# Weighing the values by half blocks of 64 keys from the fourth batch on

## The chip, the cores and the metric
One core of one Trainium2 chip. The metric is the device time of one execution in microseconds (us), the median of three runs.

## What is computed
Attention with a causal window of 128 keys and a linear bias by distance, for 8 batches, 8 heads, 576 positions and 64 features a head, and then an MLP with GELU over all 4608 positions.

```python
scores = scale * np.matmul(q, k.transpose(0, 1, 3, 2))
mask = (rel >= 0) & (rel < window)                  # window = 128, rel = query - key
scores = np.where(mask, scores + bias[None], -1000000000.0)
attn = np.exp(scores - max); attn = attn / (sum + 1e-09)
x = np.matmul(attn, v)                              # (4608, 512) after the heads are joined
h = x @ w_in                                        # 512 x 2048
return (0.5 * h * (1.0 + erf(h * inv_sqrt2))) @ w_out   # 2048 x 512
```

## The kernel before
The positions are taken in nine tiles of 512 tokens (`TT`); a batch has 576, so batch b fills the end of tile b and the beginning of tile b+1. Most products are made from pairs of 16-bit parts, high and low, in three terms: (high, high), (high, low), (low, high).

**Attention.** A unit is one batch and one pair of heads (`Unit`; four pairs a batch). Queries go in nine blocks j of 64 (`QB`), each of which sees the key blocks j-2, j-1 and j. The rows of a unit stand in nine groups (`GROUPS`): five of even blocks (`EVEN`), four of odd ones (`ODD`). `scores` (matmuls of L415) fills five PSUM banks of the ring `att`, which has four buffers; DVE (L437) reads them with the bias into `s`. `softmax` makes, for the even groups and then for the odd ones, the maximum (DVE L507), the exponential (ACT L510), the normalised weights as a high part (POOL L519) and a low part (DVE L149, the helper `low_part`) in `e_main`, and one transposing DMA on SP's queue (L522) into `et`. Weights stand in `et` as two slots of 128 keys for each group: an even block j has its keys j-2 and j-1 in slot 0, its own keys in the lower half of slot 1, and zeros in the upper half; an odd block has j-2 in the upper half of slot 0, zeros below, and j-1 and j in slot 1.

`weigh` multiplies `et` with the values. It goes over the two tiles that the batch touches (blocks 0 to 7-b for tile b, blocks 8-b to 8 for tile b+1), with one `att` bank for each. For every block of 128 keys and slot there is one matmul a head: the values are the stationary 128 rows x 64 columns, the two heads go to the two halves of the columns, and where two neighbouring blocks j share it, they go together:

```python
for slot, j0 in ((1, 2 * kb), (0, 2 * kb + 2)):
    js = [j for j in (j0, j0 + 1) if j in blocks]
```

So a unit has 54 to 66 matmuls of 128 or 64 columns (L559). Then, for each tile, ACT reads the bank into the high part of the tile `x` (L572) and DVE makes the low part (L573, at the helper's line L149).

**MLP.** `mlp_in` (L600) makes the 16 blocks of h from x, 12 matmuls each; GELU by ACT (L623) into `g32`, of the ring `ob` with three buffers; the high part by POOL (L625) and the low part by DVE (L149). `mlp_out` (L661) makes four blocks of 128 tokens, 48 matmuls each. Both use the PSUM ring `mm` of four banks.

**Order.** The main loop runs over the tiles t = 1 to 7 in 32 steps (16 of `mlp_in`, 16 of `mlp_out`) and puts the attention of batch t+1 into them: `SCORES_AT, WEIGH_AT = (2, 11, 16, 21), (12, 20, 25, 30)`. At step 24 `split_qk` splits the next q and k, at step 1 of the next tile `split_v` splits V (ACT L337, DVE L149), and the loads and maxima of the batch after (`load_v`, `stat_v`, `split_qk`; DVE L217) follow. A scheduler then sets the final order on every engine by its own model of time, so a step can end some matmuls off its place. Tile 8 is made by another scheme (`seven_all`).

Of the kernel before, what the change touches and what calls it, by code (L numbers as in the profile page):

```python
# [11 lines left out]
F32 = mybir.dt.float32  # L12
I32 = mybir.dt.int32
U32 = mybir.dt.uint32
AF = mybir.ActivationFunctionType
# [3 lines left out]
B, H, S, D = 8, 8, 576, 64  # L19
WINDOW = 128  # L20
P = 128
QB = 64
NB = S // QB
# [4 lines left out]
TT = 512  # L28
# [6 lines left out]
NKB = 5  # L35
# [13 lines left out]
NEVEN = 5  # L49
# [8 lines left out]
def attention_gelu_mlp(  # L58
# [10 lines left out]
    nc = tc.nc  # L69
    pool = ctx.enter_context(tc.tile_pool(name="sb", bufs=1))  # L70
    dram = ctx.enter_context(tc.tile_pool(name="dram", bufs=1, space=bass.MemoryType.DRAM))
    psum = ctx.enter_context(tc.tile_pool(name="ps", bufs=1, space=bass.MemoryType.PSUM))

    def small(shape, name, bufs, tag=None, dt=F32):
        return pool.tile(shape, dt, tag=tag or name, name=name, bufs=bufs)
# [8 lines left out]
    ident, upper, never = (adders[:, n] for n in range(3))  # L84
# [63 lines left out]
    def low_part(dst, src, scale, high):  # L148
        nc.vector.scalar_tensor_tensor(  # L149
            out=dst, in0=src, scalar=scale, in1=high, op0=ALU.mult, op1=ALU.subtract  # L150
        )
# [139 lines left out]
    def x_tile(t):  # L291
        if t not in xt:
            xt[t] = pool.tile([P, NCC, 2, TT], F16, tag="x", name=f"x{t}", bufs=2)
        return xt[t]
# [7 lines left out]
    vbuf = pool.tile([P, 2, NPAIR, NKB, P], F16, name="vbuf")  # L302

    pwv, scv, pwx, sx, cx = {}, {}, {}, {}, {}
# [229 lines left out]
    def weigh(st):  # L534

        b, hp, et = st.b, st.hp, st.et
        first = NB - 1 - b
        for t, blocks in ((b, range(0, first)), (b + 1, range(first, NB))):
            av = psum.tile([P, TT], F32, tag="att" if b else "mm", name=f"av{st.u}_{t}", bufs=4)
            jobs = []  # L540
            for kb in range(NKB):
                for slot, j0 in ((1, 2 * kb), (0, 2 * kb + 2)):
                    js = [j for j in (j0, j0 + 1) if j in blocks]
                    if js:
                        jobs.append((kb, slot, js))
            terms = ((None, 0),) if b < EXACT else ((0, 0), (0, 1), (1, 0))
            k = 1 if b < EXACT else 2
            todo = [(vi, ei, job) for vi, ei in terms for job in jobs]
            for n, (vi, ei, (kb, slot, js)) in enumerate(todo):
                for h in range(2):  # L550
                    r = slice(h * D, h * D + D)
                    j = js[0]
                    half = (j // 2) % 2
                    g = 4 if j == 8 else (NEVEN if j % 2 else 0) + 2 * h + j // 4
                    if j == 8:
                        half = h
                    base = et[:, (g * k + ei) * 2 + slot, half * QB : half * QB + QB]
                    steps = [[NEVEN * 2 * k * P, 2]] if len(js) == 2 else []
                    nc.tensor.matmul(  # L559
                        av[r, (j - blocks[0]) * QB : (j - blocks[0] + len(js)) * QB],  # L560
                        v32s[b][:, hp, kb, r] if b < EXACT else vbuf[:, vi, hp, kb, r],
                        bass.AP(tensor=base.tensor, offset=base.offset, ap=[list(base.ap[0])] + steps + [[1, QB]]),
                        start=(n == 0), stop=(n == len(todo) - 1), skip_group_check=True,
                    )
            n = len(blocks) * QB
            at = b * S + blocks[0] * QB - t * TT
            if b == 0 and t == 1:
                nc.scalar.copy(tail[:, hp], av[:, :n])
                continue
            x = x_tile(t)[:, hp, :, at : at + n]  # L570
            c = sx[t] if b < EXACT else cx[b, t] if t < B else cx_last
            nc.scalar.activation(x[:, 0], av[:, :n], AF.Copy, scale=c)  # L572
            low_part(x[:, 1], av[:, :n], c, x[:, 0])  # L573


    g_of = {}
# [415 lines left out]
    cx_last = None  # L992
# [5 lines left out]
    for hp in range(NPAIR):  # L998
        turn(unit(0, hp))
        if hp + 1 < NPAIR:  # L1000
            softmax_first(unit(0, hp + 1))
        if hp == 0:
            stat_v(0)
        if hp + 2 < NPAIR:
            all_scores(unit(0, hp + 2))
        weigh(unit(0, hp))
# [3 lines left out]
    for n in range(0, NWP, 2):  # L1010
        g = gates[n // 2]
# [30 lines left out]
    todo = [(m, whole, 0, NFC - 1) for m in range(NWP)]  # L1042
# [3 lines left out]
    for n, (m, tbs, first, last) in enumerate(todo):  # L1046
        for fc in (2 * m, 2 * m + 1):
            for tb in tbs:
                mlp_out(0, tb, fc, first, last)
        if n in split_at:  # L1050
            weights_out_split(split_at[n])
        if n == 2:
            stat_v(2)
        if n in scores_at:
            all_scores(unit(1, scores_at[n]))
            softmax(unit(1, scores_at[n]))
        if n in weigh_at:
            weigh(unit(1, weigh_at[n]))
# [9 lines left out]
    for t in range(1, NTILE):  # L1068
        b = t + 1
        scores_at, weigh_at = (SCORES_AT, WEIGH_AT) if t > 1 else ((8, 14, 18, 22), (17, 22, 26, 30))  # L1070
        at = {s + i: (hp, i) for hp, s in enumerate(scores_at) for i in range(3)}
# [5 lines left out]
        for step in range(2 * NFC):  # L1077
            if step < NFC:
                mlp_in(t, step)
            else:  # L1080
                tb, q = divmod(step - NFC, 4)
# [11 lines left out]
            if step in at:  # L1093
                hp, i = at[step]
# [8 lines left out]
            if step == 6:  # L1103
                if b + 1 < B:
                    stat_v(b + 1)
                else:
# [4 lines left out]
                    cx_last = small([P, 1], "cxl", 1)  # L1111
                    nc.vector.tensor_scalar(cx_last, pwv[B - 1], sx[B], 2.0 ** -27, op0=ALU.mult, op1=ALU.mult)
            if step in weigh_at:
                weigh(unit(b, weigh_at.index(step)))
# [43 lines left out]
```

## Time and profile before

| | us |
|---|---|
| median of 3 runs | 944.19 (943.04 to 946.74) |
| the profiled execution | 947.36 |
| its span, first to last instruction | 945.3 |
| PE busy | 909.2 |
| DVE busy | 720.3 |
| ACT busy | 546.5 |
| POOL busy | 194.2 |

PE's busy time is the time in which at least one matmul is under way; matmuls overlap, so it says how long PE was not idle, not how well it was used. A line number is that of the kernel; L149 is a helper that makes the low part of many tiles, which are told apart by the names beside it. Idle time of an engine other than PE counts only where PE comes to wait for it.

### The profile page before, as it was taken

The page shows a single profiled execution, that of the slowest core. Times are in us where ns is not written, and L with a number is a line of the kernel's source. Part 1 is how long each engine was busy: PE and PEld are TensorE (multiplying, and loading weights), DVE is VectorE, ACT ScalarE, POOL GpSimd, SP SyncE. Part 2 cuts the span into 40 slices and gives each one's busy share as a digit, 9 for nine tenths or more (in the row PEclk, how much of TensorE's full clock was granted, in tenths as well). Part 3 has the DMA queues.
Part 4 walks back from the last instruction along what each step waited for, and adds up shares of the span by engine and source line. Part 5 has one row for each costly group of instructions (what it writes and reads, how often), then busy time and mean ns, then how long its engine had stood idle before and what let it go on. Part 6 is the DMA issues. An engine that isn't in the chain of part 4 may idle for free.

```text
span 945.3 us, 18563 instructions
## 1 busy us (share of the span) xinstructions
PE 909.2 (96%) x7356; PEld 475.2 (50%) x7356; DVE 720.3 (76%) x1445; ACT 546.5 (58%) x1146; POOL 194.2 (21%) x412
## 2 busy tenths in 40 slices
PE   6969999789999899999999999999999999999998
PEld 3544444444454345444454445444544444445887
DVE  6798989779876877678767877787656799991771
ACT  5977967776673565356435643564465526731760
POOL 1010000013101443135313531163125420000000
PEclk9889999999999999999999999999999999999999
DMA  9518532972446124614562346225302554300201
GB/s 317 212 45 259 209 105 67 203 191 61 90 126 165 36 57 83 187 43 79 96 162 68 62 101 174 69 51 99 86 13 51 91 116 146 90 34 23 79 24 45
DMA packets 185527, 99.63 MB, mean 105 GB/s; under 512 B 133344, under 2 KB 165216, under 8 KB 185312
## 3 DMA queue, kind: packets, MB, share of 16 engines
q1 hardware_dynamic: 185440, 98.45, 41.3%
q8 instruction: 57, 0.93, 0.4%
q14 instruction: 30, 0.25, 0.1%
HBM read 50.72 MB, written 13.63 MB: 68 GB/s over the span
## 4 chain that ended last, share of the span: by engine, by line
PE 68%; DVE 7%; ACT 5%; DMA 4%; issue 2%; SPq 1%; DVEq 0%; ACTq 0%
PE o L661 31%; PE h L600 22%; PE av L559 4%; PE sc L415 4%; DMA v<-vp 2%; PE u L789 2%; PE u_out L901 2%; PE v L789 2%; DMA et<-e_main 1%; ACT s L510 1%; DVE stv L217 1%; DVE vbuf L149 1%; DVE nmax L507 1%; ACT L623 1%; ACT vbuf L337 1%
## 5 line engine op out<-in xcount | busy, mean ns | idle before, releaser
L600 PE MATMUL h<-x,wi 128*128 128x512 f16 x1536 | 344.7, 382 | 6.5 <-ACT g L623 3.0
L661 PE MATMUL o<-wo,g 128*128 128x512 f16 x1080 | 244.7, 379 | 1.1 <-DVE wo L149 1.1
L600 PEld LDWEIGHTS <-wi 128*128 128x128 f16 x1536 | 148.2, 98 | 188.0 <-issue 14.2
L661 PEld LDWEIGHTS <-g 128*128 128x128 f16 x1440 | 136.0, 98 | 164.6 <-issue 3.0
L510 ACT ACTIVATE s<-s,nmax 128x192 f32<-128x192 f32 x252 | 111.2, 443 | 103.1 <-DVE nmax L507 99.5
L623 ACT ACTIVATE g<-h,gs 128x512 f32<-128x512 f32 x112 | 74.8, 685 | 81.0 <-PE h L600 57.4
L149 DVE SCALAR_TENSOR_TENSOR g<-g,sg,g 128x512 f16<-128x512 f32 (+1 forms) x128 | 101.9, 811 | 22.6 <-POOL g L625 19.4
L625 POOL TENSOR_SCALAR g<-g,sg 128x512 f16<-128x512 f32 x96 | 78.5, 823 | 193.4 <-ACT g L623 189.6
L149 DVE SCALAR_TENSOR_TENSOR e_main<-s,z,e_main 128x192 f16<-128x192 f32 x252 | 107.4, 469 | 14.1 <-POOL e_main L519 9.6
L519 POOL TENSOR_SCALAR e_main<-s,z 128x192 f16<-128x192 f32 x180 | 87.6, 506 | 85.4 <-ACT s L510 29.0
L415 PE MATMUL sc<-kbuf,qbuf 64*64 64x192 f16 (+1 forms) x1656 | 74.3, 261 | 9.8 <-DMA kbuf<-kp 4.5
L661 PE MATMUL o<-wo_first,g 128*128 128x512 f16 x360 | 83.2, 380 | 0.3 <-DMA wo_first<-wo 0.3
L437 DVE SCALAR_TENSOR_TENSOR s<-sc,cs,bias_h 128x384 f32<-128x384 f32 x112 | 63.7, 607 | 12.8 <-PE sc L415 12.6
L507 DVE TENSOR_REDUCE nmax<-s 128x5 f32<-128x960 f32 (+1 forms) x56 | 58.5, 1044 | 2.2 <-POOL s L442 0.2
L442 POOL MEMSET s<- 64x128 f32 (+1 forms) x112 | 19.2, 172 | 186.4 <-DVE s L437 185.7
L572 ACT ACTIVATE x<-av,cx 128x448 f16<-128x448 f32 (+6 forms) x52 | 23.6, 474 | 58.4 <-PE av L559 58.2
L415 PEld LDWEIGHTS <-qbuf 64*64 64x64 f16 x1512 | 35.9, 106 | 38.2 <-issue 35.5
L559 PE MATMUL av<-et,vbuf 128*64 128x128 f16 (+1 forms) x1680 | 45.2, 213 | 4.2 <-DMA et<-e_main 4.2
L559 PEld LDWEIGHTS <-vbuf 128*64 128x64 f16 x1680 | 42.1, 113 | 14.3 <-issue 9.0
L510 ACT ACTIVATION_READ_ACCUMULATOR s<-s,nmax 128x1 f32 x252 | 47.2, 187 | 0.0
L510 ACT ACT_TABLE_LOAD x29 | 37.2, 1283 | 7.8 <-DVE square L120 7.3
L623 ACT ACT_TABLE_LOAD x29 | 37.2, 1283 | 6.4 <-issue 2.9
(224 smaller groups left out, 1029.0 us busy)
## 6 DMA issues: line engine op xcount, KB each, us to landing
v<-vp SPq DMA_DIRECT2D x32, 320.0 KB, 5.1
out<-ob SPq DMA_DIRECT2D x35, 256.0 KB, 2.2
raw<-w_in SPq DMA_DIRECT2D x8, 1024.0 KB, 14.0
raw<-w_out SPq DMA_DIRECT2D x8, 1024.0 KB, 5.7
q<-qp SPq DMA_DIRECT2D x7, 1152.0 KB, 6.1
k<-kp SPq DMA_DIRECT2D x7, 1152.0 KB, 6.6
stored<-ts SPq DMA_DIRECT2D x32, 128.0 KB, 2.2
room<-stored SPq DMA_DIRECT2D x12, 256.0 KB, 2.7
```

Of the source, the lines that this page charges most:

```text
L149: nc.vector.scalar_tensor_tensor(out=dst, in0=src, scalar=scale, in1=high, op0=ALU.mult, op1=ALU.subtract)
L415: nc.tensor.matmul(ps[bank][o, n, 0:W], a, m, start=(i == 0), stop=(i == len(terms) - 1 and b > 0), skip_group_check=True,)
L437: nc.vector.scalar_tensor_tensor(out=s[:, bank[0] : bank[0] + k, :], in0=ps[bank][:, 0:k, 0:W], scalar=cs, in1=bias.broadcast_to([P, k, W] ...
L507: nc.vector.tensor_reduce(out=nmax[:, r], in_=s[:, r], axis=AX.X, op=ALU.max, negate=True)
L510: nc.scalar.activation(s[:, i, :], s[:, i, :], AF.Exp, bias=nmax[:, i : i + 1], accum_out=z[:, i : i + 1])
L519: nc.gpsimd.tensor_scalar(e[:, i, 0, c], s[:, i], z[:, i : i + 1], 1.0, op0=ALU.mult, op1=ALU.mult)
L559: nc.tensor.matmul(av[r, (j - blocks[0]) * QB : (j - blocks[0] + len(js)) * QB], v32s[b][:, hp, kb, r] if b < EXACT else vbuf[:, vi, hp, k ...
L600: nc.tensor.matmul(ph, wi[n][:, a, cc, k * P : (k + 1) * P], x[:, cc, b, :], start=(i == 0), stop=(i == 3 * NCC - 1),)
L623: nc.scalar.activation(g32, ph, AF.Gelu, scale=gsc[t, n])
L625: nc.gpsimd.tensor_scalar(g[:, r, 0], g32, gsg[t, n], 1.0, op0=ALU.mult, op1=ALU.mult)
L661: nc.tensor.matmul(o, both[:, a, c], wo[n][:, b, k, :], start=(fc == first and i == 0), stop=(fc == last and i == 2),)
L789: nc.tensor.matmul(ps[:, k * HT : (k + 1) * HT], w(a, i)[:, k * P : (k + 1) * P], m(b, i),  start=first and n == 0, stop=True, skip_group_ ...
```

## The change
From batch 3 on, `weigh` hands over to `weigh_halves`. It leaves out the products with the zero halves. A term then has eight half products (five on the lower 64 rows, three on the upper 64 rows, each with 64 columns) and eight whole blocks of 128 keys, each for one block j of 64 columns and for both heads: 96 matmuls a unit. Half products of all three terms come first, then the whole blocks. Even j go to one bank and odd j to the other, whatever their tile, so both banks are open for the whole unit, and each tile is read out of both: four reads by ACT and four by DVE (three each in batch 7, where tile 7 has block 0 alone), with targets of every second block of 64.

```diff
+        if b >= 3:
+            weigh_halves(st, first)
+            return
...
+    def weigh_halves(st, first):
+        b, hp, et = st.b, st.hp, st.et
+        av = [psum.tile([P, TT], F32, tag="att", name=f"av{st.u}_{n}", bufs=4) for n in range(2)]
+        lower, upper, every = slice(0, QB), slice(QB, P), slice(0, P)
+        halves = []
+        for kb in range(NKB):
+            halves.append((kb, lower, 1, 2 * kb))
+            if 2 * kb + 3 < NB:
+                halves.append((kb, upper, 0, 2 * kb + 3))
+        wholes = [((j - 1) // 2, every, j % 2, j) for j in range(1, NB)]
+        terms = ((0, 0), (0, 1), (1, 0))
+        todo = [(vi, ei, job) for jobs in (halves, wholes) for vi, ei in terms for job in jobs]
+        begun = set()
+        for vi, ei, (kb, rows, slot, j) in todo:
+            for h in range(2):
+                r = slice(h * D, h * D + D)
+                half = h if j == 8 else (j // 2) % 2
+                g = 4 if j == 8 else (NEVEN if j % 2 else 0) + 2 * h + j // 4
+                nc.tensor.matmul(
+                    av[j % 2][r, j // 2 * QB : (j // 2 + 1) * QB], vbuf[rows, vi, hp, kb, r],
+                    et[rows, (2 * g + ei) * 2 + slot, half * QB : half * QB + QB],
+                    start=(j % 2, h) not in begun, stop=True, skip_group_check=True,
+                )
+                begun.add((j % 2, h))
+        for t, blocks in ((b, range(0, first)), (b + 1, range(first, NB))):
+            for n in range(2):
+                js = [j for j in blocks if j % 2 == n]
...
+                nc.scalar.activation(x[:, 0], v, AF.Copy, scale=c)
+                low_part(x[:, 1], v, c, x[:, 0])
```

The scheduler's order changes at the ends of batches. First PE at the weighing of batch 3's last pair (`av3_3`; `o2_3` is the last block of tile 2's output, `wo4` and `wo6` are weights in the order of use). Before:

```order
L661 LDWEIGHTS g2_3_3776
L661 MATMUL o2_3_4526<-wo6_1686,g2_3_3776 128x512
L559 LDWEIGHTS vbuf_84
L559 MATMUL av3_3_3_4563<-et3_3_4335,vbuf_84 64x128
L559 LDWEIGHTS vbuf_84
```

Now:

```order
L704 LDWEIGHTS g2_2_3676
L704 MATMUL o2_3_4628<-wo4_1566,g2_2_3676 128x512
L599 LDWEIGHTS vbuf_84
L599 MATMUL av3_3_0_4665<-et3_3_4403,vbuf_84 64x64
L599 LDWEIGHTS vbuf_84
```

Before, 44 of the 48 matmuls of `o2_3` stand ahead of the weighing; now 36. In batches 4 and 5 it is 45 and 44 before and 36 now; in batches 6 and 7 it is 36 both times. The first six half products of this unit are all lower ones.

Then DVE from the end of batch 3 on (`stv5` is the maximum of the next V, `s4_0` the read of the next batch's first scores, `g3_0` the low part of the next tile's first blocks). Before:

```order
L149 SCALAR_TENSOR_TENSOR x3_2758<-av3_3_3_4563,cx3_3_2304,x3_2758 128x320
L149 SCALAR_TENSOR_TENSOR vbuf_84<-v32_4_3412,scv4_3636,vbuf_84 128x2560
L149 SCALAR_TENSOR_TENSOR x4_3859<-av3_3_4_4596,cx3_4_3642,x4_3859 128x256
L642 TENSOR_SCALAR so4_5887<-pwm_1174,pwx4_3638 128x1
L149 SCALAR_TENSOR_TENSOR g3_0_4669<-g32_3_0_4670,sg3_0_4652,g3_0_4669 128x512
L149 SCALAR_TENSOR_TENSOR g3_0_4669<-g32_3_1_4687,sg3_0_4652,g3_0_4669 128x512
L217 TENSOR_REDUCE stv5_4895<-v32_5_4693 128x1
L437 SCALAR_TENSOR_TENSOR s4_0_4719<-sc4_0_0_4720,cs4_4409,bias_h_63 128x384
```

Now:

```order
L149 SCALAR_TENSOR_TENSOR vbuf_84<-v32_4_3412,scv4_3636,vbuf_84 128x2560
L149 SCALAR_TENSOR_TENSOR x3_2758<-av3_3_1_4666,cx3_3_2304,x3_2758 128x2x64
L149 SCALAR_TENSOR_TENSOR x3_2758<-av3_3_0_4665,cx3_3_2304,x3_2758 128x3x64
L685 TENSOR_SCALAR so4_6207<-pwm_1174,pwx4_3638 128x1
L149 SCALAR_TENSOR_TENSOR x4_3891<-av3_3_1_4666,cx3_4_3642,x4_3891 128x2x64
L149 SCALAR_TENSOR_TENSOR x4_3891<-av3_3_0_4665,cx3_4_3642,x4_3891 128x2x64
L217 TENSOR_REDUCE stv5_5031<-v32_5_4829 128x1
L149 SCALAR_TENSOR_TENSOR g3_0_4805<-g32_3_0_4806,sg3_0_4788,g3_0_4805 128x512
L437 SCALAR_TENSOR_TENSOR s4_0_4855<-sc4_0_0_4856,cs4_4477,bias_h_63 128x384
```

The two splits of g stood ahead of the maximum of V; now they stand behind it, the first of them ahead of the scores' read. The split of V now comes ahead of all reads of the last unit, on ACT too.

## Rows read from the trace of the kernel before

**Rows 1.** The page: PE's busy time, and its granted clock in 40 slices.
```profile
PE 909.2 (96%) x7356; PEld 475.2 (50%) x7356; DVE 720.3 (76%) x1445; ACT 546.5 (58%) x1146; POOL 194.2 (21%) x412
PEclk9889999999999999999999999999999999999999
```
**Rows 2.** Waits of PE, 250 to 865 us: us in total, times, longest.
```profile
PE h L600 <- ACT g L623: 3.0, 2, 2.4
PE sc L415 <- DVE s L437: 0.6, 1, 0.6
```
**Rows 3.** Timeline of PE, 440 to 470 us: start, length, instruction, form, count.
```profile
445.76 0.69 PE L415 MATMUL sc<-kbuf,qbuf 64*64 64x192 f16 x24
446.38 2.76 PE L661 MATMUL o<-wo,g 128*128 128x512 f16 x12
449.07 0.44 PE L415 MATMUL sc<-kbuf,qbuf 64*64 64x192 f16 x6
449.44 2.76 PE L661 MATMUL o<-wo,g 128*128 128x512 f16 x12
...
458.04 1.55 PE L559 MATMUL av<-et,vbuf 128*64 128x128 f16 x54
459.52 2.76 PE L661 MATMUL o<-wo,g 128*128 128x512 f16 x12
```
**Rows 4.** Timeline of PE, 587 to 592 us, end of batch 5.
```profile
588.48 1.60 PE L559 MATMUL av<-et,vbuf 128*64 128x128 f16 x66
590.01 1.04 PE L661 MATMUL o<-wo,g 128*128 128x512 f16 x4
```
**Rows 5.** Timelines of DVE and PE, 429 to 436 us, first pair of batch 4.
```profile
432.67 1.13 DVE L437 SCALAR_TENSOR_TENSOR s<-sc,cs,bias_h 128x384 f32<-128x384 f32 x2
...
433.08 1.55 PE L559 MATMUL av<-et,vbuf 128*64 128x128 f16 x54
```
**Rows 6.** Timeline of ACT, 683 to 706 us, reads of batch 6's last pair.
```profile
684.57 0.37 ACT L572 ACTIVATE x<-av,cx 128x128 f16<-128x128 f32 x1 [12.05 <-PE av L559]
...
687.70 0.61 ACT L572 ACTIVATE x<-av,cx 128x448 f16<-128x448 f32 x1
```
**Rows 7.** Timelines of PE, ends of batches 3 and 4; in brackets the idle time before.
```profile
392.51 1.60 PE L559 MATMUL av<-et,vbuf 128*64 128x128 f16 x66
...
410.32 0.68 PE L415 MATMUL sc<-kbuf,qbuf 64*64 64x192 f16 x15 [0.57 <-DVE s L437]
...
490.98 1.55 PE L559 MATMUL av<-et,vbuf 128*64 128x128 f16 x54
...
521.72 3.61 PE L600 MATMUL h<-x,wi 128*128 128x512 f16 x16 [0.61 <-ACT g L623]
```
**Rows 8.** Tile et, last transposes of batches 3, 4, 5: issue and time to landing.
```profile
L522 SPq DMA_TRANSPOSE et<-e_main x1: 2848/2848/2848, 387.6 to 387.6; - x1
DMA to landing us min/median/max: 4.3/4.3/4.3
...
L522 SPq DMA_TRANSPOSE et<-e_main x1: 3002/3002/3002, 485.7 to 485.7; - x1
DMA to landing us min/median/max: 4.9/4.9/4.9
...
L522 SPq DMA_TRANSPOSE et<-e_main x1: 3022/3022/3022, 583.6 to 583.6; - x1
DMA to landing us min/median/max: 4.5/4.5/4.5
```
**Rows 9.** Chain of waits, 385 to 425 us, across batch 3's end: start, length, what.
```profile
393.91 2.44 ACT vbuf L337
...
400.86 6.04 DMA v<-vp
...
406.92 2.82 DVE stv L217
...
424.13 1.02 PE h L600 x4
```

More of the change, by code (lines that the diff above doesn't have):

```diff
@@ L573, in weigh @@
             low_part(x[:, 1], av[:, :n], c, x[:, 0])
+    def weigh_halves(st, first):
[25 more added lines that the diff above has]
+                js = [j for j in blocks if j % 2 == n]
+                if not js:
+                    continue
+                v = av[n][:, js[0] // 2 * QB : (js[-1] // 2 + 1) * QB].rearrange("p (j q) -> p j q", q=QB)
+                at = (b * S - t * TT) // QB
+                x = x_tile(t)[:, hp].rearrange("p a (j q) -> p a j q", q=QB)[:, :, at + js[0] : at + js[-1] + 1 : 2]
+                c = cx[b, t] if t < B else cx_last
+                nc.scalar.activation(x[:, 0], v, AF.Copy, scale=c)
+                low_part(x[:, 1], v, c, x[:, 0])
     g_of = {}
```

## The prediction

> **What bounds the kernel now.** I read the page first: TensorE (PE) is busy for 96% of the span, at the full granted clock in nearly every slice from a quarter of the span on [rows 1]. Then the waits of PE between 250 and 865 us, where every unit of the change lies: two waits for ACT (3.0 us) are the largest entry, and with the others they come to under 4 us [rows 2]. So in this stretch a microsecond taken from PE's own stream is a microsecond of the span, and one added to DVE or ACT costs nothing unless PE comes to wait for it. Last I read the timeline of PE around the weighing of values (L559), the landing of the transposed weights that it reads, and the chain of waits across a batch's end.
>
> A unit is one batch and head pair. The change touches batches 3 to 7, four pairs each: 20 units. The timeline gives what a unit costs from its first matmul to the next line's first: 1.48 us for the 54 matmuls of batch 4 [rows 3] and 1.53 us for the 66 of batch 5 [rows 4]. Scores give the same for four products at once: 24 matmuls of 192 columns take 0.62 us to the next line, 6 of them 0.37 us [rows 3].
>
> **Prices.** The 24 scores stand in six rounds of four tiles, the 6 in three rounds of two. From 6r + e = 0.62 and 3r + e = 0.37 come r = 0.083 us a round and e = 0.12 us, the gap when PE leaves one tiling of the array for another. Four tiles thus take a round in the time of two.
> Batch 5 has 30 wide (128 columns) and 36 narrow (64) matmuls, two heads side by side: 15a + 18c + e = 1.53. Batch 4 has 42 and 12: 21a + 6c + e = 1.48. With e = 0.12 this gives about 0.056 us for a wide pair (a) and 0.032 us for a narrow pair (c).
>
> **The change part by part.**
> *Matmuls.* Before, each of a unit's three terms multiplies 16 blocks of 64 columns, all with 128 keys, in wide and narrow pairs: 1.36 to 1.41 us, and e; about 1.51 us in the mean over the 20 (batches 3 and 5 are alike, and 4 and 6; batch 7, 36 wide and 24 narrow, lies between). After, a term has 8 whole blocks and 8 half blocks, 5 on the lower 64 rows and 3 on the upper; all are narrow. If an upper half runs beside a lower one, a unit is 15 rounds of halves, a gap, 24 pairs of whole blocks, a gap. The round of four narrow products is in no row: below it is bounded by a third of the scores' round, 0.028 us, above by two narrow pairs one after the other, 0.064 us. I take 0.032, the narrow pair, since four tiles cost what two do in the scores, with the same division by rows and banks. Unit: 39 x 0.032 + 2 x 0.12 = 1.49 us. That is 0.02 us less than before: over 20 units **-0.4 us**. Three of 16 blocks are saved, but most of that goes into narrow pairs, which cost more than half a wide one, and into the second gap.
> *First pair of a batch.* There the 6 scores stand right ahead, in the tiling of the half blocks, so 0.12 us of gap goes: 5 x -0.12. But both banks are needed almost at once, where before the second bank came half a unit later, and that bank is the one that DVE's first of two L437 reads empties: at 432.67 + half of 1.13 = 433.24, against 433.08 - 0.12 when PE now arrives [rows 5]. Some 0.1 to 0.3 us of wait in three of five: **0 us** in sum.
> *Evictions.* Two reads by ACT and two by DVE become four and four (three in batch 7), with strided targets. ACT takes 0.37 us for 128 columns and 0.61 for 448 [rows 6], so a read costs some 0.27 us before its columns: 0.5 us more of ACT a unit, and DVE about 0.4. ACT's second pair now also waits for DVE to have read the same bank. I cost this at nothing, because the tiles x of these evictions are read only in the next MLP step and the banks are wanted again 5 us later; without that cover it is 20 x 0.9 us.
> *The last pair of a batch.* The order puts this weighing 8 (batch 3 and 5) or 9 (batch 4) matmuls of L661 earlier than before, at 36 of 48; in batches 6 and 7 it stood there already. Twelve of those and a gap take 2.69 us [rows 3], so one is 0.214 us and PE arrives 1.7 to 1.9 us earlier: at 390.8, 489.1 and 586.8 instead of 392.51, 490.98 and 588.48 [rows 4, 7]. The transposed weights of the odd groups land at 387.6 + 4.3 = 391.9, 485.7 + 4.9 = 490.6 and 583.6 + 4.5 = 588.1 [rows 8]. Before, that was just in time; now PE, which takes its matmuls in order, stands for 1.1, 1.5 and 1.3 us. Three rounds of lower halves go ahead of the first odd one (0.1 us each time), and in batches 4 and 5 one of DVE's splits of the weights moves up past a wait: I take 3.5 us in all. Queued behind it on PE are 12 matmuls of L661 and the next MLP step.
> Against this stand the waits that follow a batch's end in the trace: 0.57 us at 410.32 and 0.61 us at 521.72 [rows 7]. They end a chain that begins with the weighing: split of V, load of the next V, its maximum (DVE L217), scores, exponentials, then PE [rows 9]. In the change that chain starts 0.6 us earlier, but DVE has a split of g (0.75 us) ahead of the scores' reads, and another further on. A later PE finds these waits mostly gone: I take back 1.5 us. Sum: **+2.0 us**.
> *Instruction fetch and queues.* 72 more PE instructions a unit; SP's order is the same but for eight stores at batch 7's end. Nothing.
>
> **Sum.** -0.4 + 0 + 2.0 = +1.6 us. The profiled execution took 947.36 us (span 945.3); by it 949.0. It stood 3.2 us over the median of the three runs, so against the median, 944.19, the forecast is **945.8 us**.
>
> **Rivals.**
> *The halves take turns (slower).* If at 64 columns the two row halves do not run side by side, because each 64-column weight load takes the place of a matmul, nine rounds a unit cost a second 0.032 us: 20 x 0.29 = +5.8 us, 951.6 us. For it: no row shows four tiles with so few columns, and the weight loads have to keep up four to a round. Against it: the scores' rounds. It turns the result to slower once over half of those rounds are paid twice. 0.15.
> *Each matmul has its own price.* Batch 5's 66 matmuls take 1.41 us without the gap, 0.021 us each, and the 24 scores 0.021 us each. If that is a price per instruction and not per round, 96 cost 2.05 us, a unit 2.29 us: 20 x 0.78 = +15.6, 960 us. Against it: a pair of narrow ones at 0.032 is 0.016 us each. 0.03. The Trainium skill has this as a rule that speaks against the change ("TensorEngine Tiling (Array Packing)", Instruction Overhead): about 60 cycles of overhead for each matmul, and no tiling factor from a dimension that is already small. As an estimate at 2.4 GHz, 96 matmuls would be 2.4 us by that page and the sum +18 us; the trace disagrees where narrow pairs run, with 0.016 us each.
> *The pace of the stream.* If narrow rounds run at 0.028 us, as the scores' columns do, a unit is 0.16 us shorter: -3.2 us more, 942.6 us. For it: nothing but the columns; against it: the narrow pairs of today. 0.14.
> *No new wait.* If the transposed weights come a microsecond earlier too, or the wait only takes the place of the later ones, 2.0 us become about -1: 942.8 us. 0.12; with the faster pace together 939.6 us, 0.06.
>
> **How the numbers follow.** The likeliest case, 0.50, is 945.8 us, with a range of its own of 943.5 to 948. A measurement of this kernel tells a change from none at about 0.5%, 4.7 us: 939.5 to 948.9. Faster by that needs both good cases together or a gap that is smaller than I read: 0.10. Slower by that is the case of the turns, the price per matmul and a little of the likeliest case's tail: 0.20. The rest, 0.70, is the same. The range, 941 to 949.5, takes in the likeliest case, each good case alone and the turns where a part of the rounds is paid twice.
>
> **What would show it.** In the changed profile a unit should take 1.45 to 1.52 us from its first matmul to the next line. The 48 half products should take about 0.5 us of this; near 0.8 says that they take turns, near 1.0 or more that each matmul is priced. The waits of PE should list the weighing on the DMA of the transposed weights three times, about a microsecond each, at the ends of batches 3, 4 and 5, and less than now on ACT's and DVE's reads behind them. ACT's evictions should rise from 40 to 76 in these batches and no PE wait should name them. The forecast is wrong if PE waits over 2 us at a batch's end and the granted clock falls to 1.2 GHz behind it, or if a unit is below 1.40 us.

## The result and the profile after

The changed kernel takes 948.57 us (median of 7 runs, 947.72 to 950.59), the kernel before 944.19 (943.04 to 946.74): a ratio of 1.0043, 95% interval 1.0027 to 1.0059. That is 4.4 us slower, where the prediction had 1.6; the range held it.

The page answers to [rows 1]. PE is busy for less of a longer span, and its granted clock is 0.9 or more in every slice:

```profile
PE 901.2 (95%) x8076; PEld 470.5 (50%) x8076; DVE 726.7 (77%) x1481; ACT 551.2 (58%) x1182; POOL 196.7 (21%) x412
...
PEclk9999999999999999999999999999999999999999
```

The waits of PE between 250 and 865 us (in all, times, longest) answer to [rows 2]:

```profile
PE h L643 <- ACT g L666: 7.2, 5, 2.4
PE av L599 <- DMA et<-e_main: 4.1, 4, 1.6
PE av L599 <- DVE s L437: 0.3, 1, 0.3
```

3.6 us of waits became 11.6 (2.4 and 2.7 us of these lie ahead of the first changed unit). An undisturbed unit, on the other hand, is what the sum said: 96 matmuls, 1.47 us from the first to the next line (timeline of PE, start and length; compare 1.48 and 1.53 in [rows 3, 4]).

```profile
471.25 1.54 PE L599 MATMUL av<-et,vbuf 64*64 64x64 f16 x96
472.72 3.63 PE L704 MATMUL o<-wo,g 128*128 128x512 f16 x16
```

By the starts of its matmuls, the 48 half products take 0.47 us, the gap 0.12 and the 48 whole ones 0.75.

At the ends of batches 3, 4 and 5 the weighing stands for the odd transposed weights, after its first six half products (timeline of PE; in brackets the idle time before the row):

```profile
387.57 1.46 PE L599 MATMUL av<-et,vbuf 64*64 64x64 f16 x90 [0.68 <-DMA et<-e_main]
...
486.93 1.46 PE L599 MATMUL av<-et,vbuf 64*64 64x64 f16 x90 [0.88 <-DMA et<-e_main]
...
588.22 1.46 PE L599 MATMUL av<-et,vbuf 64*64 64x64 f16 x90 [1.57 <-DMA et<-e_main]
```

And some 33 us behind each of these, PE stands for ACT's gelu, which has to empty a bank; in [rows 7] the waits behind a batch's end are 0.57 and 0.61 us:

```profile
421.02 1.24 PE L643 MATMUL h<-x,wi 128*128 128x512 f16 x5 [1.46 <-ACT g L666]
...
520.44 1.89 PE L643 MATMUL h<-x,wi 128*128 128x512 f16 x8 [1.53 <-ACT g L666]
...
621.69 1.67 PE L643 MATMUL h<-x,wi 128*128 128x512 f16 x7 [1.49 <-ACT g L666]
```

**Which part to compare.** Up to the first weighing of batch 3 the programs are the same, yet that part took 328.2 to 334.7 us in the fourteen profiles of this study. So I compare the stretch from there (334.70 us before, 329.93 after) to the end of batch 7's last weighing (782.56 and 784.56): 447.9 us before, 454.6 after, +6.8. Of this 0.3 us is no time lost: the first weighing now starts among the six scores ahead of it. From starts to starts the other 6.4 us are made of: 15 units that are not the first of a batch, -0.5; five first pairs, +1.0 (three are 0.13 us shorter, two wait); the three waits for odd weights, +3.7 (0.9, 1.1 and 1.8); waits behind a batch's end, 2.8 before (1.6 of them for scores at the ends of batches 3 and 5, 1.2 for gelu) and 5.0 after (all for gelu), +2.2. (Counted so, a wait is some 0.2 us longer than in brackets, and a stretch in which scores run two at a time instead of four counts as a wait too; the expectations below count in nearly this way.)

**Why gelu comes late.** DVE's timeline behind the end of batch 3:

```profile
391.29 2.88 DVE L149 SCALAR_TENSOR_TENSOR vbuf<-v,scv,vbuf 128x2560 f16<-128x2560 f32 x1 [3.24 <-ACT vbuf L337]
394.09 0.67 DVE L149 SCALAR_TENSOR_TENSOR x<-av,cx,x 128x128 f16<-128x128 f32 x2
...
401.30 2.82 DVE L217 TENSOR_REDUCE stv<-v 128x1 f32<-128x2560 f32 x1 [5.75 <-DMA v<-vp]
404.03 0.74 DVE L149 SCALAR_TENSOR_TENSOR g<-g,sg,g 128x512 f16<-128x512 f32 x1
404.69 1.13 DVE L437 SCALAR_TENSOR_TENSOR s<-sc,cs,bias_h 128x384 f32<-128x384 f32 x2
405.75 0.74 DVE L149 SCALAR_TENSOR_TENSOR g<-g,sg,g 128x512 f16<-128x512 f32 x1
...
408.99 1.13 DVE L507 TENSOR_REDUCE nmax<-s 128x5 f32<-128x960 f32 x1
```

The split of the next V (vbuf) runs ahead of the reads of the last unit (x). So the new x is whole only at 394.8, the next step's first three blocks finish together, and DVE stands idle for 5.75 us before V's maximum with no g to split. All the splits of g then come behind it, ahead of the scores' maximum, for which ACT waits with the exponentials: 7.7 us from the start of stv to that of nmax, 6.5 before (406.92 [rows 9] to 413.43). The split passes the reads because the last products of a unit use V's low part: V's high part is free before the unit ends, while both banks are complete only at its end. Before, tile b's bank was complete half a unit earlier.

On ACT the load of the exponentials' table has come behind the same maximum (timeline of ACT). At the end of batch 3 before (second view, of ACT and DVE), it ran during the wait and nmax was followed by the exponential at once.

```profile
410.20 1.28 ACT L510 ACT_TABLE_LOAD   x1 [2.93 <-DVE nmax L507]
411.49 0.46 ACT L510 ACTIVATE s<-s,nmax 128x192 f32<-128x192 f32 x1
```

```profile
409.97 1.28 ACT L510 ACT_TABLE_LOAD   x1
413.43 1.15 DVE L507 TENSOR_REDUCE nmax<-s 128x5 f32<-128x960 f32 x1
414.61 0.46 ACT L510 ACTIVATE s<-s,nmax 128x192 f32<-128x192 f32 x1 [3.36 <-DVE square L120]
```

From the start of V's maximum to the next batch's first exponential it is 7.6 to 7.7 us at the ends of batches 3, 4 and 5 before, and 10.2 at all three now. At the ends of 3 and 5 the splits of g take 1.2 and 1.3 of these 2.5 us, the table load 1.3 at each; at the end of 4, where the load stood behind the maximum before too, all 2.5 come on DVE. So two things delay the exponentials, and the runs below have to be read for both.

### The profile page after: what moved, and what is told of

Its sections match the earlier page's. It is cut to its first block, busy times and chain, and to the rows that moved or that the text cites. A ratio compares the mean times of both kernels' runs of the same rounds, so it can differ in the third digit from the quotient of the medians.

```text
span 947.3 us, 20059 instructions
## 1 busy us (share of the span) xinstructions
PE 901.2 (95%) x8076; PEld 470.5 (50%) x8076; DVE 726.7 (77%) x1481; ACT 551.2 (58%) x1182; POOL 196.7 (21%) x412
## 4 chain that ended last, share of the span: by engine, by line
PE 45%; DMA 5%; DVE 5%; ACT 2%; issue 2%; POOL 1%; SPq 0%; DVEq 0%; POOLq 0%; ACTq 0%
PE o L704 18%; PE h L643 15%; PE sc L415 2%; PE av L599 2%; PE u L832 2%; DMA et<-e_main 2%; DMA q<-qp 2%; PE u_out L944 2%; PE v L832 2%; DMA v<-vp 1%; DVE e_main L149 1%; DVE kbuf L149 1%; ACT s L510 1%; DVE s L437 1%; DVE g L149 1%
## 5 line engine op out<-in xcount | busy, mean ns | idle before, releaser
L643 PE MATMUL h<-x,wi 128*128 128x512 f16 x1536 | 340.7, 379 | 11.2 <-ACT g L666 7.2
L668 POOL TENSOR_SCALAR g<-g,sg 128x512 f16<-128x512 f32 x96 | 81.1, 851 | 200.3 <-ACT g L666 197.9
L149 DVE SCALAR_TENSOR_TENSOR e_main<-s,z,e_main 128x192 f16<-128x192 f32 x252 | 110.3, 483 | 10.3 <-POOL e_main L519 5.7
L337 ACT ACTIVATE vbuf<-v,scv 128x2560 f16<-128x2560 f32 x7 | 17.0, 2433 | 45.3 <-PE av L599 45.3
L217 DVE TENSOR_REDUCE stv<-v 128x1 f32<-128x2560 f32 x8 | 22.5, 2818 | 22.6 <-DMA v<-vp 22.6
L615 ACT ACTIVATE x<-av,cx 128x128 f16<-128x128 f32 (+3 forms) x68 | 21.9, 366 | 28.7 <-DVE x L149 25.2
```

The lines of the kernel that those rows point to most:

```text
L149: nc.vector.scalar_tensor_tensor(out=dst, in0=src, scalar=scale, in1=high, op0=ALU.mult, op1=ALU.subtract)
L217: nc.vector.tensor_reduce(out=dst, in_=src, axis=axis, op=ALU.max, apply_absolute_value=True)
L643: nc.tensor.matmul(ph, wi[n][:, a, cc, k * P : (k + 1) * P], x[:, cc, b, :], start=(i == 0), stop=(i == 3 * NCC - 1),)
L668: nc.gpsimd.tensor_scalar(g[:, r, 0], g32, gsg[t, n], 1.0, op0=ALU.mult, op1=ALU.mult)
```

## The experiments

Theory A: the loss lies in the order at a batch's end, above all the split of V that goes first. Rival B: a chain that starts at the weighing ends the batch, and PE's gains are only waited away. Rival C: the half products or the doubled reads cost the time themselves. The stretch is the one defined above, of the profiled execution; the waits (us, 325 to 865) are as the view of PE's waits lists them. In 2, 6 and 11 the stretch ends with six more matmuls of `mlp_out` ahead of batch 7's last weighing (1.3 us), in 4 with three (0.6): that comes with the edit and is no loss. The kernel before also waits 0.6 us for scores, 12 waits 1.3.

| kernel | median us | ratio to before, 95% | stretch us | waits for odd weights | for gelu |
|---|---|---|---|---|---|
| before | 944.19 | | 447.9 | 0 | 0.6 |
| changed | 948.57 | 1.0043 (1.0027 to 1.0059) | 454.6 | 4.1 | 4.5 |
| 1 low part of V second | 948.08 | 1.0046 (1.0031 to 1.0062) | 451.9 | 4.7 | 1.7 |
| 2 weighing at 42 | 950.66 | 1.0080 (1.0062 to 1.0099) | 456.7 | 2.2 | 6.0 |
| 3 old kernel, tiles turned | 950.15 | 1.0070 (1.0048 to 1.0092) | 453.6 | 0.2 | 5.3 |
| 4 low part second, at 39 | 942.60 | 0.9989 (0.9968 to 1.0009) | 449.1 | 2.4 | 0 |
| 5 as 1, early table | 950.09 | 1.0064 (1.0044 to 1.0085) | 455.6 | 6.5 | 1.0 |
| 6 low part second, at 42, early table | 941.83 | 0.9989 (0.9970 to 1.0009) | 448.6 | 1.6 | 0 |
| 7 middle pairs only | 943.21 | 1.0001 (0.9985 to 1.0016) | 448.2 | 2.0 | 1.1 |
| 8 halves apart | 951.62 | 1.0085 (1.0059 to 1.0111) | 457.8 | 4.3 | 3.9 |
| 9 weights first | 951.53 | 1.0083 (1.0062 to 1.0103) | 458.5 | 6.9 | 2.2 |
| 10 as 5, weights first | 950.96 | 1.0074 (1.0046 to 1.0102) | 453.0 | 4.5 | 2.0 |
| 11 as 6, weights first | 943.66 | 1.0000 (0.9983 to 1.0018) | 447.8 | 1.6 | 0 |
| 12 old kernel, weights first | 944.35 | 1.0001 (0.9986 to 1.0016) | 449.1 | 0 | 0.8 |

The kernel before had medians of 943.88 (beside 1 to 4), 942.93 (5 to 8) and 943.47 (9 to 12).

### 1. V's low part second

```diff
-        terms = ((0, 0), (0, 1), (1, 0))
+        terms = ((0, 0), (1, 0), (0, 1))
```

> The changed kernel with its three terms in another order: the products with V's low part (vi=1) come second instead of last, so that V's high part is read to the unit's end. Nothing else is edited; the sum is the same but for the order of its parts. Theory A (the split of V goes first): in the changed kernel V's high part is free 16 whole products before the end of the last weighing of a batch, while its evictions can only start at the end; so the split of V (2.9 us on DVE) stands ahead of the last evictions, the first three blocks of the next MLP step finish together and late, DVE's splits of g fall behind V's maximum, and the scores' exponentials come late. Here the evictions are ahead again. The three waits of PE for ACT's gelu behind the ends of batches 3, 4 and 5, 4.9 us together in the changed kernel, fall to 1.5 to 3.5; the waits for the transposed odd weights stay at about 3.5 us. Time 945 to 947. Theory B (PE is merely early: what ends the wait is a chain that starts at the weighing, however DVE is ordered): the gelu waits stay within 0.5 us of 4.9, time 948 to 949.5. Theory C (the unit's stream or the doubled reads cost the time, the waits only show it): time 948 to 949.5 too, with smaller gelu waits and the time coming back elsewhere.

DVE's timeline behind the end of batch 3 in this kernel:

```profile
389.85 0.73 DVE L149 SCALAR_TENSOR_TENSOR x<-av,cx,x 128x128 f16<-128x128 f32 x2 [1.31 <-ACT x L615]
392.48 2.88 DVE L149 SCALAR_TENSOR_TENSOR vbuf<-v,scv,vbuf 128x2560 f16<-128x2560 f32 x1 [1.90 <-ACT vbuf L337]
...
398.03 0.75 DVE L149 SCALAR_TENSOR_TENSOR g<-g,sg,g 128x512 f16<-128x512 f32 x1 [2.02 <-POOL g L668]
399.38 0.75 DVE L149 SCALAR_TENSOR_TENSOR g<-g,sg,g 128x512 f16<-128x512 f32 x1 [0.60 <-POOL g L668]
402.49 2.82 DVE L217 TENSOR_REDUCE stv<-v 128x1 f32<-128x2560 f32 x1 [2.36 <-DMA v<-vp]
...
408.71 1.14 DVE L507 TENSOR_REDUCE nmax<-s 128x5 f32<-128x960 f32 x1
```

The reads of x are ahead of the split again, two splits of g lie in the wait for V, and from stv to nmax it is 6.2 us instead of 7.7. The waits for gelu fall as theory A has it, 4.5 to 1.7 us, and the stretch by 2.8. From V's maximum to the first exponential it is 8.7 us instead of 10.2: DVE's part of the delay is gone, the table load still stands behind the maximum. The time does not fall with it: 948.08, above theory A's range. So the larger part of the gelu waits is shown to come of V's split, but this repair alone gains nothing that the runs can tell; why the median does not follow the stretch of the profiled execution stays open.

### 2. The last weighing after 42 of 48

```diff
+                    if step == 31 and fc == 13 and 3 <= b < B:
+                        weigh(unit(b, NPAIR - 1))
...
-            if step in weigh_at:
+            if step in weigh_at and not (b >= 3 and step == 30):
```

> The changed kernel, with the last pair's weighing in batches 3 to 7 put into the order after 42 of the 48 matmuls of L704 instead of 36. PE arrives 1.3 us later at the odd transposed weights, so the waits there (0.8, 1.0 and 1.7 us at the ends of batches 3, 4, 5) fall to 0, 0 and 0.4. If waits add up (theory C, each stall is a cost of its own), the time falls by about 3 us, to 945.5. If the end of each batch is set by a chain from the weighing over V's split, its load and maximum, scores and exponentials to gelu (theories A and B), that chain starts no earlier, PE only comes to it earlier, and the waits for gelu grow from 4.9 to 7 to 8.5 us: time 948 to 949.5, no gain.

```profile
PE h L643 <- ACT g L666: 6.0, 3, 2.0
PE av L599 <- DMA et<-e_main: 2.2, 2, 1.3
```

The waits for weights halve, those for gelu grow by 1.5 us (2 to 3.5 were expected), and the kernel is 2 us slower than the changed one, slower than any theory had it. The waits alone would make it 0.4 us faster. The edit also changed PE's order: at the ends of batches 3 to 6 the next batch's first 24 scores now stand in two pieces with three matmuls of h between, some 1.2 us in all; another 1.3 us of the stretch are the six matmuls at its end. So most of what is not waited for at the weighing is waited for 33 us later, with V's split in the wrong place. This speaks against C, and does not tell A from B.

### 3. The old kernel with V's split passing the reads

```diff
-        for t, blocks in ((b, range(0, first)), (b + 1, range(first, NB))):
+        both = ((b, range(0, first)), (b + 1, range(first, NB)))
+        for t, blocks in (both[::-1] if b >= 3 and hp == 3 else both):
```

> The kernel before, with no half products: in the last pair of batches 3 to 7 alone, the two x tiles of a unit are weighed in the other order (b+1 first). The same matmuls, evictions and reads; but V's high part is free while the eviction that the next MLP block reads is the last. Theory A: the split of V passes that eviction, the first three blocks finish together, and behind the ends of batches 3, 4 and 5 PE waits for gelu as in the changed kernel: 3 to 5 us in sum instead of 1.2 to 1.8, time 946 to 948. Theory B and C: no change beyond 1 us, 943.5 to 945.2, since PE arrives as before and nothing is added.

```profile
PE h L601 <- ACT g L624: 5.3, 3, 2.4
PE av L560 <- DMA et<-e_main: 0.2, 1, 0.2
```

No half product, no second bank, no read more: and waits for gelu at the same three ends, with a loss of 0.7%, more than that of the change and than theory A had. B and C fall as the whole explanation. The loss is not that of V's split alone, though. The table load now stands behind the maximum at all three ends, where it stood at one, and PE takes the next batch's first scores in two or three pieces (timeline of PE behind the end of batch 3; they were 24 in a row):

```profile
399.16 0.36 PE L415 MATMUL sc<-kbuf,qbuf 64*64 64x192 f16 x8
399.45 0.82 PE L601 MATMUL h<-x,wi 128*128 128x512 f16 x3
400.20 0.52 PE L415 MATMUL sc<-kbuf,qbuf 64*64 64x192 f16 x16
```

From starts to starts the stretch grows by 5.7 us: waits for gelu +4.7, waits for scores behind a batch's end -1.5, the scores in pieces some +1.6, first pairs and last weighings +0.9.

### 4. Both orders mended

The edits of 1 and of 2, with `fc == 12` in place of 13.

> The changed kernel with the order of terms of the first experiment and the last pair's weighing after 39 of 48 matmuls; in this order the table load ahead of the first exponentials of batches 4, 5 and 6 (1.28 us on ACT) no longer carries the wait for DVE's maximum, so it can run while ACT waits. Theory A: the waits for the odd transposed weights fall from 3.5 to about 1.6 us, those for gelu from 4.9 to 0.5 to 2; the time is 941.5 to 944, at or below the kernel before by the shorter units (20 x 0.036 = 0.7 us). Theory B: waits for gelu 4 to 5 us, time 947 to 949. Theory C: the waits fall but the time stays over 946.

```profile
PE av L599 <- DMA et<-e_main: 2.4, 3, 1.4
PE av L599 <- DVE s L437: 0.4, 1, 0.4
```

942.60 us, 6 us less than the changed kernel, with all the 96-matmul units, second banks and doubled reads in it; the two intervals do not touch. A third thing has changed with the two edits, as the expectation says: the table load runs ahead of the maximum again, at all three ends (timeline of ACT behind the end of batch 3), and from V's maximum to the first exponential it is 7.6 us, as before the change.

```profile
405.35 1.28 ACT L510 ACT_TABLE_LOAD   x1
408.56 0.46 ACT L510 ACTIVATE s<-s,nmax 128x192 f32<-128x192 f32 x1 [1.93 <-DVE nmax L507]
```

What the change lost, it lost by the order at a batch's end; this run does not say how much of it by V's split, by the load and by the early weighing.

### 5. and 6. One exponential more, meant to take the table load out of the chain

```diff
+        if st.hp == 0 and st.b >= 4:
+            early = small([P, 1], f"early{u}", 2, tag="early")
+            with tc.high_priority(EXP_AHEAD):
+                nc.scalar.activation(early, s[:, 4, 0:1], AF.Exp)
```

in the kernel of 1 (weighing at 36) and in that of 4 with the weighing at 42.

> The first experiment's kernel (V's low part second), and one more exponential of a single column ahead of the first exponentials of batches 4 to 7, on a score that DVE has written 1.2 us before the maximum is there; its result is used by nothing. The order on PE and DVE stays as in the first experiment. ACT's table load for exponentials (1.28 us) then runs while ACT waits for the maximum instead of behind it. If the load behind the maximum is part of what PE waits for, the three gelu waits fall from 2.2 us together to under 0.7, and the time from 948.1 to 945.5 to 947. If the load is hidden anyway, the waits stay at 2.2 us and the time at 948.

> The fourth experiment's kernel with the last pair's weighing after 42 instead of 39 of 48 matmuls, and the early exponential of one column, so that the table load is covered in spite of another order on DVE. Theory A: the wait for the odd transposed weights at the end of batch 5 falls from 1.4 to 0.8 us and those of batches 3 and 4 (0.13 and 0.2 us) go; the waits for gelu stay under 1 us together: 941 to 942.5, against 942.6. If the chain from the weighing to gelu takes back what a later weighing gives, the waits for gelu grow to 1.5 to 3 us and the time is 943 to 945.

5 is a miss, and the edit does not do what it was made for. A gelu stands between the early exponential and the others, so ACT changes its table twice more, and the exponentials' load is again the last thing ahead of them, behind the maximum (timeline of ACT behind the end of batch 3 in 5; nmax ends at 411.86):

```profile
406.76 1.28 ACT L509 ACT_TABLE_LOAD   x1
410.12 0.20 ACT L509 ACTIVATE early<-s 128x1 f32<-128x1 f32 x1 [2.07 <-DVE s L437]
410.34 1.28 ACT L670 ACT_TABLE_LOAD   x1
411.63 0.69 ACT L670 ACTIVATE g<-h,gs 128x512 f32<-128x512 f32 x1
412.34 1.28 ACT L514 ACT_TABLE_LOAD   x1
413.63 0.45 ACT L514 ACTIVATE s<-s,nmax 128x192 f32<-128x192 f32 x1
```

From V's maximum to these exponentials it is 9.0 us, 8.7 in 1. So 5 and 6, and 10 and 11 that are made from them, say nothing of what the load costs. The waits for gelu fall from 1.7 to 1.0 us, while PE waits longer for weights, 6.5 us: at the end of batch 3, ahead of the first early exponential, the weighing stood for 2.1 us where it stood 0.6 in 1, because the even weights took 9.0 us to land, 7.5 in 1, and the odd ones were issued 1.4 us later behind them. PE and DVE have the same order in 1 and 5, so this much is scatter of single executions. 6 is as theory A has it in time and in waits, but with the load behind the maximum: there DVE reads the scores ahead of V's maximum, and from that to the exponentials it is 6.9 us. In 5 and 6 the weighing differs by six matmuls, 1.3 us of PE, and by this order of DVE; the times differ by 8 us, the stretches by 7.0: 4.9 us of waits for weights, 1.0 for gelu, and seven matmuls in 5 that take 0.4 us each instead of 0.21, behind waits of over 2 us. So with V's split mended the early weighing still loses. Six matmuls at three ends are at most 3.9 us of it; the rest I lay to the transfers of this execution, which no run shows.

### 7. Middle pairs only

```diff
-        if b >= 3:
+        if b >= 3 and hp in (1, 2):
```

> Half products only in the second and third pair of batches 3 to 7 (10 units); the first and last pair of each are weighed as before, so neither the banks behind the scores nor the end of a batch are touched. If the losses lie at the two ends of a batch alone, what is left is 10 units at 1.47 instead of 1.51 us: 0.4 us faster than before, 943 to 944.2, with no wait over 1 us that the kernel before doesn't have. If the doubled reads of ACT and DVE or the narrow matmuls cost time anywhere else, it is slower than before by 1 to 3 us: 945 to 947.

943.21 us, no difference. Ten units of half products, with their reads, cost nothing that the runs can tell; nor can they tell the gain of about 0.4 us. The order put the last weighing after 42 of 48 by itself, and at the end of batch 5 there are two waits over 1 us that the expectation did not have: 1.8 us for odd weights and, behind it, 1.1 for gelu. The second one is the nearest the runs come to a price of the table load. V's split is behind the first read of x at the ends of batches 3, 4 and 5 alike; at 3 and 4 the load runs ahead of the maximum, from V's maximum to the exponentials it is 7.6 us, and gelu is waited for 0.1 us. At 5 the load stands behind it, the 7.6 us become 8.8, and the wait is there:

```profile
604.12 1.28 ACT L510 ACT_TABLE_LOAD   x1 [3.24 <-DVE nmax L507]
```

### 8. Halves apart

```diff
-        todo = [(vi, ei, job) for jobs in (halves, wholes) for vi, ei in terms for job in jobs]
+        low, high = ([job for job in halves if job[1] is rows] for rows in (lower, upper))
+        todo = [(vi, ei, job) for jobs in (low, high, wholes) for vi, ei in terms for job in jobs]
```

> The changed kernel with the half products of a unit in another order: all on the lower 64 rows first (15 pairs), then all on the upper (9 pairs), so that lower and upper can't run side by side. If the changed kernel runs four half products at once, a unit of 1.47 us becomes 1.47 + 9 x 0.032 = 1.76 us; part of the 20 x 0.29 = 5.8 us is covered where PE waits anyway: 951 to 954.5. If the halves take turns already, the unit stays at 1.47 us and the time at 948 to 949.

```profile
472.86 1.73 PE L600 MATMUL av<-et,vbuf 64*64 64x64 f16 x96
474.52 1.68 PE L705 MATMUL o<-wo,g 128*128 128x512 f16 x7
```

1.66 us a unit, 0.19 more: in the changed kernel the halves do run four at once. It is less than 0.29 because the two kinds still meet: rounds of two start 0.031 us apart, as the mixed rounds of four do (0.47 over 15), but where the lower products end and the upper begin, fourteen products start within 0.1 us. Six rounds more are left of the nine: 6 x 0.031 = 0.19.

### 9. to 12. The splits of the weights ahead of the next queries' maximum

DVE's maximum of the next queries waits for their load, and the last three splits of the weights stand behind it. I took that for the cause of the late odd weights.

```diff
+                    if b >= 3 and hp == NPAIR - 1:
+                        landed[b] = small([P, 1], f"landed{b}", 2, tag="landed")
+                        nc.vector.tensor_copy(landed[b], e_main[:, NG - 1, 1, 255:256])
...
-                split_qk(b + 1)
+                split_qk(b + 1, landed.get(b - 1))
```

in the changed kernel (9), in 5 (10), in 6 (11) and in the kernel before (12).

> The changed kernel, with DVE's maximum of the next queries (stq, 2.55 us, which waits for their load) held back until DVE has split the last weights of a batch; a copy of one element does this. The matmuls and their order on PE, and the split of V ahead of the last evictions, stay. If the odd transposed weights are late because the last three splits stand behind that load and that maximum, the waits at the ends of batches 3, 4 and 5 go from 3.5 us to under 0.5, the last weighing ends earlier, and with it V's split and all that follows; the three waits for gelu then stay at 4 to 5.5 us. Time 945 to 947. If the transposing transfer itself is the limit, the waits stay above 2.5 us and the time at 948 to 949.

> The fifth experiment's kernel (V's low part second, early table load; the weighing after 36 of 48) with the splits of the weights ahead of the next queries' maximum as in the ninth. If the two places are all that the half products lost, the waits for odd weights at the ends of batches fall under 0.5 us and those for gelu to 1 to 2 us: 942 to 943.5, and no half-clock stretch behind them. If PE's gain is taken back by the chain through V's load and maximum, the gelu waits grow to 3 us or more: 944 to 946.

> The sixth experiment's kernel (V's low part second, early table load, the weighing after 42 of 48) with the splits of the weights ahead of the next queries' maximum. The wait for odd weights at the end of batch 5, 0.7 us there, goes; the gelu waits stay under 1 us: 940.5 to 942. If the load of the next queries, now later seen by DVE, delays the next batch's scores, a new wait of scores of 1 us or more appears behind a batch's end and the time is 943 or more.

> The kernel before with that one edit alone: the splits of the last weights ahead of the next queries' maximum, no half products. The kernel before has no wait for the transposed weights at these places, so nothing is to be gained: 943 to 944.5. If it gains 1 us or more, what the tenth and eleventh experiment gain is not owed to the half products.

9 and 10 are misses, and the theory behind them falls: the waits for weights stay at 6.9 and 4.5 us. At the end of batch 5 the odd transfer is issued 13.9 us after the start of the last scores in 9 and 16.4 in the changed kernel, but lands 22.9 after it, not 21.8. From the chains of waits, the changed kernel first (start, length):

```profile
582.81 5.36 DMA et<-e_main
```

```profile
580.67 8.97 DMA et<-e_main
```

In 9 it is issued right behind the load of the next keys and runs beside it; in both kernels some 3.8 MB move in the 22 us from 370 us on. Whether the bytes or the transposing itself set its pace was not tried. In the changed kernel the odd weights land 20.9, 21.1 and 21.8 us after the start of the last scores of the batch; PE reaches the weighing 20.0 us after it with 36 matmuls ahead, 21.3 with 42 and 21.8 with 44. That is the whole of the wait for weights.

9 also shows what a long wait can bring behind it. Windows at the end of batch 4 (length, busy time and count of PE, PEld, DVE, ACT, POOL, then the granted clock):

```profile
486.90:488.50 1.60, 1.60 (x91) 1.35 (x92) 0.62 (x1) 0.42 (x1) 0.00 (x0) 0.95 0.00 0
488.50:491.50 3.00, 3.00 (x8) 1.03 (x7) 0.96 (x1) 2.52 (x3) 0.00 (x0) 0.50 0.02 5
```

PE had stood for 1.64 us ahead of the weighing; just behind it the granted clock is 0.50, the level of 1.2 GHz, for seven matmuls of 0.43 us instead of 0.21: 1.5 us, and as much again at the end of batch 5. Not every such wait does this: behind 1.76 us at the end of batch 3 in 9 itself, and behind 2.35 at the end of batch 5 in 1, the clock stays at 1.00. In the changed kernel's profile, with 0.88 us of wait at this place, it stays at 1.00 too; its other runs are not profiled.

11 and 12 are level with the kernel before, 12 as expected, 11 above its 940.5 to 942: its waits for odd weights stay at 1.6 us. Of 11 the profiled execution was short (447.8 us of stretch), the median is not: no version beats the kernel before by more than the interval. 4 and 6 come nearest, 0.1% below it.

## Why the prediction was right and wrong

**Units: right.** -0.4 us forecast, -0.5 measured; 1.47 us a unit against 1.49, four halves at once. That a round of four costs what a round of two does was put into the two equations for the scores, not got from them; the gap of 0.12 us and the rounds of 0.031 bear it out. The rivals of turns and of a price per matmul fall: 0.47 us for 48 halves is 0.010 us each. By the Trainium skill ("TensorEngine Tiling (Array Packing)", Instruction Overhead) each matmul has about 60 cycles of overhead; as a price of each of these matmuls the trace disagrees, and the time did not rise for that reason.

**First pair of a batch: too low.** 0 forecast, +1.0 measured. Three pairs gain the 0.13 us; batch 3 waits 0.35 us for the bank, as the text allowed, and batch 5 waits 0.99 us for transposed weights, which it did not see.

**Waits at the last pair: right.** 3.5 us forecast; 3.7 measured between starts, at the three places named. Moving the weighing back shortens them (runs 2, 4, 6).

**"I take back 1.5 us": this step failed.** The text said that a later PE finds the old waits behind a batch's end mostly gone. They grew from 2.8 to 5.0 us: +2.2 where the sum has -1.5. The prediction had the facts ahead of it: the order shown there has the split of V ahead of the reads, and two splits of g behind V's maximum. It priced them as one or two splits of 0.75 us on a chain that starts earlier, and took the reads of the last unit as not urgent ("read only in the next MLP step"): for the last pair that step is the next thing PE does. It also has no term for the table load that came behind the maximum. V's maximum did start earlier at two of the three ends (by 1.4 and 0.5 us, counted against PE's matmuls), but from there to the exponentials it took 10.2 us instead of 7.7. Run 3 shows that V's split ahead of the reads, with the orders that came with it, costs 0.7% in the old kernel; run 1 that mending V's split takes the gelu waits from 4.5 to 1.7; run 7 that the load alone is worth about 1.1 us where it stands behind the maximum.

**Doubled reads: right.** Nothing forecast; nothing seen in run 7, and run 4 is level with all of them in.

**The range: held by luck.** 948.57 us lies outside the 943.5 to 948 of the likeliest case. The upper end, 949.5, was there for halves that take turns in a part of the rounds, which they do not; the result came there by the step that failed.

The sum of the sizes found, +6.4 us in the stretch, is over the 4.4 us between the medians; I take the difference for the scatter of single executions, whose early parts alone lie 6.5 us apart.

## What to carry to other kernels

When work is regrouped so that results come complete only at the end, ask what was released in the middle before: here a buffer became free ahead of the results, its refill passed their reads, and the loss came 33 us later on two other engines. Where the order of instructions moves, price the new order on the engine that feeds the next stage, and do not set an earlier start of a chain against a later bound without walking the chain. And mend such waits together: each repair alone moved the loss elsewhere (runs 1, 2), both together took it away (run 4, where the table load went back to its old place as well). Take from its trace what a repair did to the order before reading its time: runs 2 and 3 changed PE's order too, and 5 left the load in the chain.

## What the hardware showed unexpectedly

By the records, half products start between the six scores that stand ahead of them in the program (timeline of PE at the first pair of batch 4):

```profile
429.61 0.27 PE L415 MATMUL sc<-kbuf,qbuf 64*64 64x192 f16 x2
429.63 0.21 PE L599 MATMUL av<-et,vbuf 64*64 64x64 f16 x1
429.71 0.24 PE L415 MATMUL sc<-kbuf,qbuf 64*64 64x192 f16 x2
429.72 0.21 PE L599 MATMUL av<-et,vbuf 64*64 64x64 f16 x1
```

Both use tiles of 64 by 64, and a tile that the scores leave idle takes the next product of its own. The Trainium skill ("TensorE: Matmul & The Clock Gate", Part 3: Packing small matmuls) has matmuls start and end strictly in program order; these starts differ from that.

A gap of 0.12 us when PE leaves one tiling for another stood in every unit, between halves and wholes too. And the transposing transfer of the odd weights, always of the same size, took 4.3 us at the end of batch 3 before and 9.0 at the end of batch 5 in 9, where it ran beside the load of the next keys; whether that load is the reason was not tried.
